# Where rows are turned in a two-layer mixture-of-experts kernel: TensorE transposes or VectorE block transposes

## The chip, the cores and the metric

One core of one Trainium2 chip runs the whole program. The metric is the device time of one execution in microseconds (us). The kernel before took 477.64 us (median of 3 runs, 476.07 to 478.81).

## The reference

```python
def reference(**kwargs):
    attn_out = _attn_ref(q, k, v, alpha)          # (2, 8, 768, 48): a gated linear recurrence
    x = attn_out.transpose(0, 2, 1, 3).reshape(B * S, H * D)        # 1536 rows of 384
    x = _moe_ref(x, w_gate, w1, w2, capacity)     # layer 1: one of 8 experts a row
    return _moe2_ref(x, w_gate, w_noise, noise, w1, w2)             # layer 2: two of 8 experts a row

def _moe_ref(...):      # per expert e, over the rows that chose it (at most 384, in order)
    out[i] = gate_w[i] * (np.maximum(x[i] @ w1[e], 0) @ w2[e])      # 384 -> 1024 -> 384

def _moe2_ref(...):     # noisy logits, the two largest, softmax of those two
    noisy_logits = logits + np.log1p(np.exp(x @ w_noise)) * noise
    out[mask] += top2_w[mask, k, None] * (np.maximum(x[mask] @ w1[e], 0) @ w2[e])
```

## The kernel before, in words

The program has three stages: the recurrence with layer 1's routing, 8 jobs of layer 1 (one per expert, numbered 0 to 7 here and `n` in the code), and 8 jobs of layer 2 (8 to 15; `E` is 8). A job is sixteen steps long. In the first eight, `hidden(n, f)` (L649) makes one block of 128 hidden units: nine products on TensorE (six in L657, three in L660: every operand is kept as a high and a low part), then ScalarE's and VectorE's high and low parts of the result (L662, L663). In the last eight, `second(n, f)` (L668, products in L686) multiplies those blocks by the second weight matrix; 72 products in all. A `hidden` result lives in one of three PSUM tiles `ph`, and is free when L662 and L663 have read it.

Beside these steps other work is issued from the same loop (L1161 on), in an order fixed by hand; there is no scheduler, so every engine runs its instructions in program order. It is:

- `raw` (L483) lets SyncE (SP) load weights two halves ahead (L492, L495), and `split` (L498) makes high and low parts of them: high on ScalarE (L510), low (L511) on VectorE or GpSimd (POOL) as `ENGS` says. `split_rest` issues the low parts one step later.
- `load_x(n)` (L572) loads the rows of job n from the store that the routing of the layer before filled by scatter (L157). `split_x(n, d)` (L597) turns a third of them, d = 0 to 2, so that features lie on partitions, and makes high and low parts. `XS` names the steps f of the second half of the job before at which this is done.
- For jobs that `turned(n)` (L559) names, which are 1 to 7 and 10 to 15, the four loads of L592 bring 32-row blocks on four groups of partitions, VectorE's 32x32 block transpose (L605) finishes the turn, and the first weight matrix is read in a copy with its rows in block order (`w1_1b`, `w1_2b`, prepared with the inputs). For the others, which are 8 and 9 (job 0 has its own way), TensorE transposes 128x128 pieces (L616) after one plain load (L569, L570). The few routing columns of a row come by a load of their own (L570, L569).
- `job_route2` and `route2` (L801, L691) route layer 2: after layer 1's job n they run in steps of the generator during job n+1, as `STEPS` says. The rank of a row among its expert's rows comes from five small products (L781 to L784, two tiles of 120 rows), then VectorE's L787 to L798, then four scatters by GpSimd.
- `finish2` (L853) ends a job of layer 2. For jobs that `turned_out(n)` (L555) names, 9 to 13, VectorE turns the result in blocks (L867), 16 loads from SBUF to SBUF by SyncE gather rows (L872), ScalarE weighs a tile of rows (L876) and GpSimd adds it to the output. For job 8 TensorE turns it back (L893).
- Rows that job 6 and 7 send late to expert 0 of layer 2 are not in job 8's block. `load_late` (L898) fetches up to 128 of them when job 7's scatters have landed, and `late_tokens` (L903) takes them through the whole expert: TensorE transposes (L908), 18 products (L920), transposes (L933), 24 products (L945). `AFTER` is the order in which the steps of `finish2(8)` (f), of `late_tokens` (l) and of `split_x(9)` (x) stand between job 8 and job 9.

```python
XS = ("135", "024", "567")     # layer 1, layer 2, job 7
AFTER = "flfflllxlxxl"
```

Of the kernel before, what the change touches and what calls it, by code (L numbers as in the profile page):

```python
# [11 lines left out]
AF = mybir.ActivationFunctionType  # L12
# [13 lines left out]
CL = 128  # L26
# [30 lines left out]
WG = 8  # L57
STEPS = ("0111122111110000", "1232210200000000", "0100000111100000", "0111000000000000")
ENGS = ("VGGGGGGGGVVVVVGV", "GGGGGGGGGGGGGGGG")
XS = ("135", "024", "567")  # L60
LATE_F = 3
AFTER = "flfflllxlxxl"
SAFE = 1e-18
LOW1, LOW2, LOW3 = C1 - 128, C2 - 128, C2 - 256

# [1 line left out]
def body(tc, ap, cap, dbg=False, stop=False):  # L67
    nc = tc.nc
    V, A, G, PE = nc.vector, nc.scalar, nc.gpsimd, nc.tensor
    with ExitStack() as ctx:  # L70
# [483 lines left out]

        def turned_out(n):  # L555

            return n > E and not by_row(n)

        def turned(n):  # L559

            return jobs[n][0] == 1 and n > 0 or place(n) is not None

        def load_rows(eng, g, rows_, c, cols):

# [7 lines left out]
        def load_x(n, eng):  # L572
            layer, e = jobs[n]
            nt_, p, c = dims(n)
            store = (xs1, xs2)[layer - 1]
            if not turned(n):
                g = sb([p, nt_, RW], "b6", 5)
                load_rows(eng, g, lambda a, b: store[e * R + a:e * R + b], c, slice(None))
            else:
                nb = -(-c // 32)  # L580
                rows_of = lambda eng, r: store[e * R:e * R + r] if layer == 1 else store[bass.ds(expert(n, eng) * R, r), :]
                w = RW if layer == 1 else RW - DM
                t6 = sb([128, nb * ND * 32 + nt_ * w], "b6", 5)
                g = t6[:p, nb * ND * 32:].rearrange("p (t d) -> p t d", t=nt_)
                if layer == 2:
                    g = few_of(g)
                load_rows(eng, g, lambda a, b: rows_of(eng.engine, nt_ * p)[a:b], c if layer == 1 else nb * 32,
                          slice(DM, None))
                x = xr_[n] = t6[:, :nb * ND * 32].rearrange("p (t d) -> p t d", t=nb)
                rows_ = rows_of(mybir.EngineType.SP, nb * 32)  # L590
                for b in range(4):
                    nc.sync.dma_start(x[b * 32:b * 32 + 32], rows_.rearrange("(t j) d -> j t d", j=32)[  # L592
                        :, :, b * ND * 32:(b + 1) * ND * 32])
            xg[n] = g
            xsp[n] = (xb([128, ND, c], F32R), xb([128, ND, c], F32R))
# [95 lines left out]
        def route2(g, yT, spare, base):  # L691
# [85 lines left out]
            V.tensor_reduce(g[:, :, NZ:NZ + E], both(wt_), axis=AX.X, op=ALU.add)  # L777
            yield
            rv = by_t(hold(nt_ * E))
            for t in range(nt_):  # L780
                PE.matmul(rv[:, t, :], tri[:p, :p], ob[:, t, :], start=True, stop=False)  # L781
                for u_ in range(t):
                    PE.matmul(rv[:, t, :], ones[:p, :p], ob[:, u_, :], start=False, stop=False)
                PE.matmul(rv[:, t, :], ones[:, :p], acc2, start=False, stop=True)  # L784
            yield
            rs = by_t(hold(nt_ * E))
            V.tensor_tensor(rs, rv, base[:p, None, :].to_broadcast(sh), op=ALU.add)  # L787
# [61 lines left out]
        def by_row(n):  # L849

            return range(3) if place(n) is not None and dims(n)[2] == 384 else None

        def finish2(n):  # L853
            nt_, p, c = dims(n)
            yp = yps.pop(n)
            if by_row(n):
                ix, ysc, group = tokens_of(xg[n], yp[0]), sb([p, nt_, DM], "b6", 5), []
                yield
                for t in range(nt_):
                    weigh(own[n], t, yp[t][:, :DM], ix, ysc, group)  # L860
                    yield
                return
            if turned_out(n):
                nb = -(-c // 32)
                z, w = sb([128, nb, ND * 32], "b6", 5), sb([128, nt_, DM], "b6", 5)
                for d in range(ND):
                    V.transpose(z[:, :, d * 32:d * 32 + 32], yp[d][:, :nb * 32].rearrange("p (t j) -> p t j", j=32))  # L867
                ix, group = tokens_of(xg[n], yp[0]), []
                yield
                for b in range(4):  # L870
                    for q in range(4):
                        nc.sync.dma_start(w[q * 32:q * 32 + 32, :len(range(q, nb, 4)), b * 96:b * 96 + 96],  # L872
                                          z[b * 32:b * 32 + 32, q::4, :])
                yield
                for t, sl, r in tiles(n):
                    A.activation(w[:r, t, :], w[:r, t, :], AF.Copy, scale=own[n][:r, t, :])  # L876
                    indirect(out, ix[:r, t:t + 1], w[:r, t, :], group, ALU.add)
                    yield
                return
            yT = sb([128, ND, c], "b6", 5)  # L880
            for d in range(ND):
                if d == 1:
                    V.tensor_copy(yT[:, d, :], yp[d][:, :c])
                else:
                    A.activation(yT[:, d, :], yp[d][:, :c], AF.Copy)
            ix = tokens_of(xg[n], yp[0])
            ysc = sb([p, nt_, DM], "b6", 5)
            yield
            group = []
            for t, sl, r in tiles(n):  # L890
                bp = ph() if n == E else pm()
                for d in range(ND):
                    PE.transpose(bp[:r, d * 128:(d + 1) * 128], yT[:, d, sl], ident)  # L893
                weigh(own[n], t, bp[:r, :DM], ix, ysc, group)
                yield


        def load_late(eng):  # L898
            g = hb([CL, 1, RW])
            eng.dma_start(g[:, 0, :], xs2[C0:C0 + CL])  # L900
            return g

        def late_tokens(n, g):  # L903

            xh, xl = xb([128, ND, CL], F32R), xb([128, ND, CL], F32R)
            xp = pm()
            for d in range(ND):
                PE.transpose(xp[:, d * CL:(d + 1) * CL], g[:, 0, d * 128:(d + 1) * 128], ident[:CL, :CL])  # L908
            m = lambda x: x.rearrange("p d c -> p (d c)")
            A.activation(m(xh), xp[:, :ND * CL], AF.Copy)  # L910
            V.tensor_tensor(m(xl), xp[:, :ND * CL], m(xh).bitcast(F32), op=ALU.subtract)
# [32 lines left out]
                for k, (l, r) in enumerate(((hh, wh), (hh, wl), (hl, wh))):  # L944
                    PE.matmul(y, l[:, sl], r, start=(f == 0 and k == 0), stop=(f == NF - 1 and k == 2))  # L945
            ysc = hb([CL, 1, DM])
            weigh(g[:, :, NZ:NZ + 1], 0, y, tokens_of(g), ysc, [])
            yield


# [214 lines left out]
        for n, (layer, e) in enumerate(jobs):  # L1165
# [3 lines left out]
            for f in range(NF):  # L1169
# [1 line left out]
                split_rest()  # L1171
                step(prev, int(steps[f]))
                if f == (3 if n == E - 1 else 0) and n not in (E, 2 * E - 1):
                    load_x(n + 1, nc.gpsimd)
                if f == 3 and turned_out(n):
                    yps[n] = {d: py() for d in range(ND)}
                    for y in yps[n].values() if dims(n)[2] % 32 else ():
# [12 lines left out]
            if n < 2 * E - 1:  # L1190
                for f in range(NF):
                    if n == E and f == LATE_F:
                        for _ in prev:
                            pass
                        g = load_late(nc.sync)
                        load_x(n + 1, nc.sync)
                        raw(n + 2, 0)
                        it = late_tokens(n, g)
                    xs_ = XS[2 if n == E - 1 else layer - 1]
                    if n != E and str(f) in xs_:  # L1200
                        split_x(n + 1, xs_.index(str(f)))
# [2 lines left out]
                        own_sums.pop()()  # L1204
                    split_rest()
                    step(prev, int(steps[8 + f]))
                    if n == E and f == 0:
                        order(2, acc2)
                    if f % 4 == 2 and (n, f) != (E, 2):
                        raw(n + 2, f // 4)  # L1210
# [15 lines left out]
                for o in AFTER if n == E else ():  # L1226
                    if o == "x":
                        split_x(n + 1, d)
                        d += 1
                    else:  # L1230
                        step(prev if o == "f" else it)
            else:
# [230 lines left out]
```

## Time and profile before

| what | value |
|---|---|
| runs | 477.64 us median, 476.07 to 478.81 |
| profiled execution | 473.87 us, its span 472.2 us |
| TensorE products (PE) | 456.6 us busy, 97% of the span, 3374 instructions |
| TensorE weight loads (PEld) | 428.6 us, 91% |
| GpSimd (POOL) | 333.0 us, 71% |
| VectorE (DVE) | 288.9 us, 61% |
| ScalarE (ACT) | 263.3 us, 56% |
| mean granted TensorE clock | 0.995 of full speed |

A busy share is an average over three stages with different limits. Times in rows are us from the start of the span. A row of a timeline gives start, duration, engine, line, operation, the tile written and the tiles read, how many instructions of that kind were merged, and in square brackets how long the engine had been idle and who released it.

### The profile page before, as it was taken

What the parts mean: (1) busy time and instruction counts of PE and PEld (TensorE: products, weight loads), DVE (VectorE), ACT (ScalarE), POOL (GpSimd) and SP (SyncE); (2) the same over time, 40 slices, a digit from 0 to 9 for tenths busy, and PEclk for the clock granted to TensorE, in tenths of its full rate; (3) what the DMA queues carried; (4) which work ended last, traced back from release to release, by engine and by line L of the source; (5) the groups of instructions that cost most, each with busy time, mean ns of one, the idle gap of its engine ahead of it and who ended that gap; (6) DMA issues with size and microseconds to landing.
All of it is one profiled execution on the core that took longest, in us unless ns stands there. A gap on an engine that the chain in (4) does not pass through costs nothing.

```text
span 472.2 us, 9805 instructions
## 1 busy us (share of the span) xinstructions
PE 456.6 (97%) x3374; PEld 428.6 (91%) x3374; DVE 288.9 (61%) x905; ACT 263.3 (56%) x683; POOL 333.0 (71%) x424
## 2 busy tenths in 40 slices
PE   8999999999999999999899999999999999999992
PEld 3688888899999999999898799999999999999992
DVE  7999988566887888888865334333442433332440
ACT  3477778377676676675553347356372555653510
POOL 3435497574777796796668219988979898696952
PEclk9999999999999999999999999999999999999997
DMA  8973863789989897786552883539377592956253
GB/s 293 408 241 143 320 235 107 254 258 307 311 307 243 264 302 219 201 290 206 175 199 59 249 210 74 122 69 336 74 254 158 142 270 55 297 104 178 37 61 48
DMA packets 73418, 95.41 MB, mean 202 GB/s; under 512 B 31261, under 2 KB 56142, under 8 KB 73358
## 3 DMA queue, kind: packets, MB, share of 16 engines
q1 hardware_dynamic: 66094, 80.54, 55.5%
q0 software_dynamic: 7264, 14.15, 12.8%
q8 instruction: 28, 0.46, 0.4%
q14 instruction: 32, 0.26, 0.2%
HBM read 70.72 MB, written 20.65 MB: 194 GB/s over the span
## 4 chain that ended last, share of the span: by engine, by line
PE 78%; DVE 11%; issue 3%; ACT 2%; DMA 2%; POOL 1%; SPq 0%; POOLq 0%; DVEq 0%
PE py L686 32%; PE ph L657 20%; PE ph L660 10%; DVE h L663 2%; PE pm L367 2%; PE ph L291 2%; DVE s L511 2%; PE py L338 2%; PE py L344 2%; PE pm L714 2%; PE py L318 1%; PE ph L920 1%; DMA s<-qs 1%; PE py L945 1%; PE py L285 1%
## 5 line engine op out<-in xcount | busy, mean ns | idle before, releaser
L511 POOL TENSOR_TENSOR s<-s,s 128x384 fp32r<-128x384 f32 x188 | 198.0, 1161 | 23.4 <-ACT s L510 19.0
L686 PE MATMUL py<-h,s 128*128 128x240 f32 (+5 forms) x1008 | 147.4, 305 | 0.0
L686 PEld LDWEIGHTS py<-h,s 128*128 128x128 f32 x1008 | 142.6, 189 | 1.3
L657 PE MATMUL ph<-x,s 128*128 128x240 f32 (+6 forms) x768 | 134.4, 310 | 0.8 <-ACT x L643 0.6
L510 ACT ACTIVATE s<-s 128x384 fp32r<-128x384 f32 x256 | 125.0, 516 | 3.9 <-DMA s<-w 2.5
L657 PEld LDWEIGHTS ph<-x,s 128*128 128x128 f32 x768 | 116.7, 189 | 2.7 <-ACT x L643 1.0
L663 DVE SCALAR_TENSOR_TENSOR h<-ph,h 128x240 fp32r<-128x240 f32 (+6 forms) x128 | 62.0, 485 | 84.8 <-ACT h L662 83.7
L662 ACT ACTIVATE h<-ph 128x240 fp32r<-128x240 f32 (+6 forms) x128 | 55.4, 433 | 79.8 <-PE ph L660 79.5
L660 PE MATMUL ph<-x,s 128*128 128x240 f32 (+6 forms) x384 | 76.8, 308 | 0.0
L157 POOL DMA_INDIRECT out<-b,m_ix x29 | 45.0, 1552 | 32.5 <-ACT b L876 7.7
L660 PEld LDWEIGHTS ph<-x,s 128*128 128x128 f32 x384 | 61.2, 189 | 0.4
L157 POOL DMA_INDIRECT xs<-b,m_si x32 | 33.8, 1057 | 21.6 <-DVE pm L797 13.7
L511 DVE TENSOR_TENSOR s<-s,s 128x384 fp32r<-128x384 f32 x68 | 48.0, 712 | 0.3 <-issue 0.2
L300 POOL TENSOR_SCALAR_AFFINE_SELECT h<-h 128x512 f32<-128x512 f32 x24 | 23.0, 980 | 27.4 <-ACT h L299 27.3
L609 DVE TENSOR_TENSOR x<-pm,x 128x240 fp32r<-128x240 f32 (+5 forms) x39 | 18.8, 482 | 26.3 <-ACT x L608 26.3
L608 ACT ACTIVATE x<-pm 128x240 fp32r<-128x240 f32 (+5 forms) x39 | 16.6, 426 | 21.0 <-DVE pm L605 17.6
L686 PE MATMUL py<-s,h 128*128 128x384 f32 x144 | 25.8, 338 | 0.0
L686 PEld LDWEIGHTS py<-s,h 128*128 128x128 f32 x144 | 25.2, 188 | 0.0
L867 DVE STREAM_TRANSPOSE b<-py 128x416 f32<-128x416 f32 (+1 forms) x15 | 8.8, 630 | 22.8 <-PE py L686 22.8
L605 DVE STREAM_TRANSPOSE pm<-b 128x256 f32<-128x256 f32 (+3 forms) x39 | 20.5, 526 | 0.0
L238 DVE TENSOR_TENSOR s<-s,s 112x256 f32<-112x256 f32 (+2 forms) x24 | 19.3, 824 | 1.4 <-DMA s<-qs 0.8
L155 POOL MEMSET spacer<- 1x1 f32 x74 | 20.1, 272 | 0.1
(253 smaller groups left out, 541.4 us busy)
## 6 DMA issues: line engine op xcount, KB each, us to landing
s<-w SPq DMA_DIRECT2D x28, 768.0 KB, 6.4
s<-w_2b SPq DMA_DIRECT2D x22, 768.0 KB, 6.6
s<-w_1b SPq DMA_DIRECT2D x14, 768.0 KB, 6.9
xs<-s SPq DMA_DIRECT2D x2, 1576.0 KB, 7.5
out<-s SPq DMA_DIRECT2D x4, 768.0 KB, 8.3
b<-xs SPq DMA_DIRECT2D x28, 96.0 KB, 6.3
b<-xs SPq DMA_DIRECT2D x12, 156.0 KB, 6.0
b<-b SPq DMA_DIRECT2D x52, 36.0 KB, 1.9
```

The source lines that it names most:

```text
L155: G.memset(spacer, 0.0)
L157: st = G.indirect_dma_start(out=dst, out_offset=bass.IndirectOffsetOnAxis(ap=ix, axis=0), in_=src, in_offset=None, **kw)
L238: eng.tensor_tensor(o, src[:, h].rearrange("r (s j) -> r s j", j=64), x[:, h].rearrange("r (s j) -> r s j", j=64), op=ALU.mult)
L300: G.affine_select(a_, a_, pattern=[[0, 4], [1, 128]], compare_op=ALU.is_ge, fill=0.0, base=0, channel_multiplier=-1)
L510: A.activation(hi[sl], t[sl], AF.Copy)
L511: rest.append(lambda: (eng or V).tensor_tensor(lo[sl], t[sl], hi[sl].bitcast(F32), op=ALU.subtract))
L605: V.transpose(y.rearrange("p (t j) -> p t j", j=32), x)
L657: PE.matmul(p, w, x[:, d, :], start=(k == 0), stop=False)
L660: PE.matmul(p, w1_of(n, f, d)[0], xl[:, d, :], start=False, stop=(d == ND - 1))
L662: A.activation(hh, p, AF.Relu)
L663: V.scalar_tensor_tensor(hl, p, 0.0, hh.bitcast(F32), op0=ALU.max, op1=ALU.subtract)
L686: PE.matmul(out_, l, r, start=(f == 0 and k == 0), stop=(f == NF - 1 and k == 2))
```

## The change

- `turned(n)` is true for every job but 0, so jobs 8 and 9 are loaded in blocks and turned by VectorE. `turned_out` takes job 8 in as well, so its result is turned by VectorE and gathered by 16 loads. Late rows are loaded by four block loads and one for their routing columns, and VectorE turns them.
- `load_x` for jobs 1 to 8 gives the load of the routing columns to SyncE (before: GpSimd).
- `split_x(8)` stands at steps 2, 4 and 6 of job 7's second half (before: 5, 6, 7).
- The five rank products of `route2` become three: one over both tiles with `tri`, one for the second tile, one over both with the running count.
- `order(2, acc2)` stands one step later in job 8, and `AFTER` is another string.

```diff
-XS = ("135", "024", "567")
+XS = ("135", "024", "246")
-AFTER = "flfflllxlxxl"
+AFTER = "llflfllxxxl"
...
-            return n > E and not by_row(n)
+            return n >= E and not by_row(n)
...
-            return jobs[n][0] == 1 and n > 0 or place(n) is not None
+            return n > 0
...
-            for t in range(nt_):
-                PE.matmul(rv[:, t, :], tri[:p, :p], ob[:, t, :], start=True, stop=False)
-                for u_ in range(t):
-                    PE.matmul(rv[:, t, :], ones[:p, :p], ob[:, u_, :], start=False, stop=False)
-                PE.matmul(rv[:, t, :], ones[:, :p], acc2, start=False, stop=True)
+            PE.matmul(rv, tri[:p, :p], ob, start=True, stop=False)
+            for t in range(nt_ - 1):
+                PE.matmul(rv[:, t + 1:, :], ones[:p, :p], ob[:, t:t + 1, :].to_broadcast([p, nt_ - 1 - t, E]),
+                          start=False, stop=False)
+            PE.matmul(rv, ones[:, :p], acc2[:, None, :].to_broadcast([128, nt_, E]), start=False, stop=True)
...
         def load_late(eng):
-            g = hb([CL, 1, RW])
-            eng.dma_start(g[:, 0, :], xs2[C0:C0 + CL])
-            return g
+            g, x, rows_ = hb([CL, 1, RW - DM]), hb([128, CL // 32, ND * 32]), xs2[C0:C0 + CL]
+            for b in range(4):
+                eng.dma_start(x[b * 32:b * 32 + 32], rows_.rearrange("(t j) d -> j t d", j=32)[
+                    :, :, b * ND * 32:(b + 1) * ND * 32])
+            eng.dma_start(g[:, 0, :], rows_[:, DM:])
+            return few_of(g), x
...
             for d in range(ND):
-                PE.transpose(xp[:, d * CL:(d + 1) * CL], g[:, 0, d * 128:(d + 1) * 128], ident[:CL, :CL])
+                V.transpose(xp[:, d * CL:(d + 1) * CL].rearrange("p (t j) -> p t j", j=32), x[:, :, d * 32:d * 32 + 32])
...
-            weigh(g[:, :, NZ:NZ + 1], 0, y, tokens_of(g), ysc, [])
+            A.activation(ysc[:, 0, :].rearrange("p (b d j) -> p d b j", b=4, d=ND),
+                         y.rearrange("p (d b j) -> p d b j", b=4, d=ND), AF.Copy, scale=g[:, 0, NZ:NZ + 1])
+            indirect(out, tokens_of(g)[:, 0:1], ysc[:, 0, :], [], ALU.add)
...
-                    load_x(n + 1, nc.gpsimd)
+                    load_x(n + 1, nc.sync if n < E else nc.gpsimd)
...
-                    if n == E and f == 0:
+                    if n == E and f == 1:
                         order(2, acc2)
...
                     if o == "x":
                         split_x(n + 1, d)
+                        split_rest()
                         d += 1
+                        while d == ND and rest:
+                            split_rest()
```

SyncE's queue around job 7, before: the second weights of job 8 (`s_687`, `s_708`), the first and then the second weights of job 9, and the late rows. The rows of job 8 were loaded from GpSimd's queue.

```order
L492 DMA s_667_3603<-w_2 128x3x512
L495 DMA s_687_3694<-w_2 128x4x384
L495 DMA s_708_3786<-w_2 128x4x384
L492 DMA s_720_3860<-w_2 128x3x512
L492 DMA s_726_3935<-w_2 128x3x512
L495 DMA s_746_4036<-w_2b 128x4x384
L495 DMA s_767_4127<-w_2b 128x4x384
L900 DMA h_4213<-xs_65 128x394
```

The same place with the change:

```order
L492 DMA s_667_3591<-w_2b 128x3x512
L495 DMA s_687_3682<-w_2b 128x4x384
L569 DMA b_691_3702<-xs_65 64x10
L570 DMA b_691_3702<-xs_65 128x2x10
L592 DMA b_691_3702<-xs_65 32x10x96 x4
L495 DMA s_708_3778<-w_2b 128x4x384
L492 DMA s_721_3853<-w_2b 128x3x512
L492 DMA s_727_3924<-w_2b 128x3x512
L495 DMA s_746_4020<-w_2b 128x4x384
L495 DMA s_770_4117<-w_2b 128x4x384
L901 DMA h_4199<-xs_65 32x4x96 x4
```

Six loads of job 8's rows, which read the store that the scatters fill, now stand on SyncE's queue between the two halves of job 8's second weights.

ScalarE's queue from the late rows' results to job 9's first blocks, before (`ysc` of job 8 is `b_787`; L844 weighs a tile out of PSUM):

```order
L936 ACTIVATE h_4338<-pm_4333 128x512
L620 ACTIVATE x_4219<-pm_4342 128x432
L936 ACTIVATE h_4354<-ph_4349 128x512
L620 ACTIVATE x_4219<-pm_4358 128x432
L620 ACTIVATE x_4219<-pm_4365 128x432
L844 ACTIVATE h_4397<-py_4372,h_4213 128x384
L844 ACTIVATE b_787_4282<-ph_4407,b_691_3714 48x384
L662 ACTIVATE h_4424<-ph_4414 128x432
```

The same place with the change (`b_793` is the tile that the 16 loads of L872 fill):

```order
L939 ACTIVATE h_4334<-pm_4329 128x512
L939 ACTIVATE h_4343<-ph_4338 128x512
L608 ACTIVATE x_4213<-pm_4347 128x432
L608 ACTIVATE x_4213<-pm_4350 128x432
L608 ACTIVATE x_4213<-pm_4354 128x432
L950 ACTIVATE h_4384<-py_4359,h_4198 128x3x4x32
L876 ACTIVATE b_793_4290<-b_793_4290,b_691_3702 128x384
L662 ACTIVATE h_4407<-ph_4397 128x432
```

In front of job 9's first L662, where ScalarE weighed a tile out of PSUM, it now weighs one that lies in SBUF and that 16 loads must have filled.

## Rows read from the trace of the kernel before

**Rows 1.** The page, its parts 1 and 2: busy time, and the granted clock.

```profile
PE 456.6 (97%) x3374; PEld 428.6 (91%) x3374; DVE 288.9 (61%) x905; ACT 263.3 (56%) x683; POOL 333.0 (71%) x424
...
PEclk9999999999999999999999999999999999999997
```

**Rows 2.** Timeline of TensorE, second half of job 7 to job 8's first block.

```profile
230.22 0.17 PE L781 MATMUL pm<-accs,tri 120*120 120x8 bf16 x1
...
230.47 2.26 PE L686 MATMUL py<-h,s 128*128 128x240 f32 x18
...
236.00 0.60 PE L616 MATMUL pm<-iw,b 128*128 128x128 f32 x3 [1.46 <-DVE accs L798]
...
239.26 1.00 PE L657 MATMUL ph<-x,s 128*128 128x304 f32 x6
...
240.52 1.64 PE L714 MATMUL pm<-iw,b 128*120 128x144 f32 x12
```

**Rows 3.** Timeline of GpSimd in the same stretch.

```profile
226.56 0.58 POOL L569 DMA_DIRECT2D b<-xs  x1 [2.15 <-issue]
...
227.93 5.88 POOL L511 TENSOR_TENSOR s<-s,s 128x384 fp32r<-128x384 f32 x6
```

**Rows 4.** Timeline of VectorE in the same stretch.

```profile
230.29 4.40 DVE L511 TENSOR_TENSOR s<-s,s 128x384 fp32r<-128x384 f32 x2
234.62 0.17 DVE L787 TENSOR_TENSOR pm<-pm,eb 120x16 f32<-120x16 f32 x1
...
235.69 0.17 DVE L798 CAST accs<-pm 120x8 bf16<-120x8 f32 x1
...
236.66 0.54 DVE L511 TENSOR_TENSOR s<-s,s 128x384 fp32r<-128x384 f32 x1
```

**Rows 5.** Groups by line and shape on VectorE: the block transposes.

```profile
L605 DVE STREAM_TRANSPOSE pm<-b 128x256 f32<-128x256 f32 x21 | 9.5, 453 | 0.0
...
L605 DVE STREAM_TRANSPOSE pm<-b 128x416 f32<-128x416 f32 x9 | 5.6, 617 | 0.0
```

**Rows 6.** Line L592, the block loads: duration of an issue on SyncE, time to landing.

```profile
L592 SPq DMA_DIRECT2D b<-xs x52: 311/450/5372, 95.2 to 408.7; - x52
...
DMA to landing us min/median/max: 2.4/7.8/13.0
```

**Rows 7.** Timeline of TensorE, from job 7's rank products to job 9's fourth block.

```profile
251.74 0.17 PE L781 MATMUL pm<-accs,tri 120*120 120x8 bf16 x1 [0.16 <-DVE m_wt L776]
...
263.19 0.52 PE L908 MATMUL pm<-iw,h 128*128 128x128 f32 x3 [0.21 <-DMA h<-xs]
...
264.29 4.58 PE L920 MATMUL ph<-s,x 128*128 128x512 f32 x18
...
270.72 1.40 PE L616 MATMUL pm<-iw,b 128*128 128x128 f32 x8 [0.31 <-DVE h L937]
272.05 4.49 PE L945 MATMUL py<-s,h 128*128 128x384 f32 x24
...
276.62 1.42 PE L657 MATMUL ph<-x,s 128*128 128x432 f32 x6
...
282.00 1.34 PE L657 MATMUL ph<-x,s 128*128 128x432 f32 x6
```

**Rows 8.** Timeline of SyncE: the load of the late rows.

```profile
260.57 0.35 SPq L900 DMA_DIRECT2D h<-xs  x1
```

**Rows 9.** Timeline of ScalarE and of VectorE: an L662, an L924 and an L663.

```profile
278.66 0.53 ACT L662 ACTIVATE h<-ph 128x432 fp32r<-128x432 f32 x1 [0.85 <-PE ph L660]
...
267.22 0.42 DVE L924 TENSOR_SCALAR h<-ph 128x256 f32<-128x256 f32 x1 [1.88 <-ACT h L926]
...
279.22 0.61 DVE L663 SCALAR_TENSOR_TENSOR h<-ph,h 128x432 fp32r<-128x432 f32 x1 [5.26 <-ACT h L662]
```

**Rows 10.** Timeline of SyncE: the sixteen loads L872 after job 9.

```profile
305.90 10.39 SPq L872 DMA_DIRECT2D b<-b  x16
```

**Rows 11.** The page, its part 6: such loads, KB each, time to landing.

```profile
b<-b SPq DMA_DIRECT2D x52, 36.0 KB, 1.9
```

More of the change, by code (lines that the diff above doesn't have):

```diff
@@ L580, in load_x @@
                 nb = -(-c // 32)
-                rows_of = lambda eng, r: store[e * R:e * R + r] if layer == 1 else store[bass.ds(expert(n, eng) * R, r), :]
+                rows_of = lambda eng, r: store[e * R:e * R + r] if layer == 1 else store[e * R:e * R + r] if place(n) is None else store[bass.ds(expert(n, eng) * R, r), :]
                 w = RW if layer == 1 else RW - DM
@@ L890, in finish2 @@
             for t, sl, r in tiles(n):
-                bp = ph() if n == E else pm()
+                bp = pm()
                 for d in range(ND):
@@ L898, in load_late, with late_tokens @@
         def load_late(eng):
-            g = hb([CL, 1, RW])
-            eng.dma_start(g[:, 0, :], xs2[C0:C0 + CL])
-            return g
-        def late_tokens(n, g):
+            g, x, rows_ = hb([CL, 1, RW - DM]), hb([128, CL // 32, ND * 32]), xs2[C0:C0 + CL]
[4 more added lines that the diff above has]
+            return few_of(g), x
+        def late_tokens(n, g, x):
             xh, xl = xb([128, ND, CL], F32R), xb([128, ND, CL], F32R)
@@ L1197, in body @@
                         raw(n + 2, 0)
-                        it = late_tokens(n, g)
+                        it = late_tokens(n, *g)
                     xs_ = XS[2 if n == E - 1 else layer - 1]
```

## The prediction
> **What bounds the kernel now.** I read the page first, for which engine is never idle; then TensorE's timeline through the two places that the change rewrites; then the timelines of the engines that feed it there. TensorE is busy for 456.6 of the 472.2 us, and its granted clock is at the upper of its two levels (2.4 GHz) in all slices but the last [rows 1]. So an instruction taken off TensorE is worth its own duration, unless something else becomes late in its place; work taken off GpSimd, VectorE or SyncE is worth nothing by itself. The places are these. At the end of job 7 TensorE turns job 8's rows in three groups of three transposes, and before the second it waits 1.46 us for VectorE; job 8's first block runs from 239.26 to 240.52 [rows 2]. VectorE was late because two of its L511 took 4.40 us beside six L511 of GpSimd [rows 3, 4] (one takes 0.54 elsewhere), and GpSimd had bunched those six because it had stood until 226.56 before it could load job 8's rows, which job 5's scatters write. Between jobs 8 and 9 TensorE first waits 0.21 us for the late rows, and then runs transposes, the late rows' products and job 9's transposes almost without a gap [rows 7].
>
> **The change, part by part.**
>
> *Rank products.* Five take 230.47 - 230.22 = 0.25 us [rows 2]; three should take 0.15. That is 0.10 us in each of 8 jobs, 0.8 in all, 0.7 of it before job 8. I expect no change of VectorE's work behind them.
>
> *Row loads of layer 1 on SyncE, seven issues off GpSimd.* Nothing waits for GpSimd there, and SyncE gets one more issue of some 0.45 us [rows 6] a job, ahead of four that wait for the same data. Cost and gain nothing; if this cover were gone, SyncE's weight loads would come 0.45 us later in a job of 18 us.
>
> *Job 8's rows.* Removed from TensorE: nine transposes (0.6 us for three at most, so 1.6) and the 1.46 us wait. With the 0.7 from above, job 8's first block could end at 240.52 - 1.46 - 1.6 - 0.7 = 236.8, a gain of 3.8; this is the upper end. Added is a chain on other engines. The loads still have to wait for job 5's scatters: 226.56 [rows 3], less 0.5 for five jobs' shorter ranks, so 226.1. SyncE issues six at 0.45, the last at 228.35. Landing took 2.4 us at least and 7.8 in the median [rows 6]. I take 2.5, since the large weight load of this moment now stands behind these loads; so the rows are there at 230.85, while the first block turn is asked for near 228.6, and VectorE's queue stands for two microseconds. From then, in the order of the program, it has: three block turns at 0.52 (between 0.453 for 256 columns and 0.617 for 416, [rows 5]), six low parts at some 0.5 [rows 4], the routing's small steps from L787 to L798, 1.24 us [rows 4], then a high part on ScalarE, a last low part and a last product, 1.1 together. The sum is 1.56 + 3.0 + 1.24 + 1.1 = 6.9 us, and job 8's first block ends at 237.75, which is 2.8 us earlier than now. With a landing of 7.8 it would end at 243.05, 2.5 us later than now; this is the lower end. The second half of job 8's second weights stands behind these loads on SyncE and lands about when its first high part is wanted; I count nothing for it. GpSimd does not bunch any more, so I expect VectorE's 4.40 us to go.
>
> By the Trainium skill, "VectorE: DVE Perf Modes", section "Rules for kernel authors", a 128x128 transpose belongs on TensorE where a PSUM destination will do, which speaks against the change. By that rule the turns would stay on TensorE and only the 0.8 us of the ranks would be gained; here TensorE is the engine without slack, so I follow the rows.
>
> *Late rows.* I count from the start of job 7's rank products (251.74 now), since the scatters and what follows them hang on those. The late load is issued 8.83 us after it (260.57, [rows 8]), and the first wide product starts 12.55 us after it (264.29, [rows 7]). With the change four loads go out, the last 1.35 us after the first, and land 2.5 after that; three turns of 128 columns take 0.32 each (the slope of [rows 5]), and the high part 0.5. The first wide product starts at 8.83 + 1.35 + 2.5 + 0.96 + 0.5 = 14.15, so 1.6 us later than now, with TensorE idle for over 3 us before it. After it the fifteen transposes of jobs 8 and 9 are gone (eight take 1.33 us, [rows 7], so 2.5), and the products wait about 0.8 us for VectorE, which turns job 8's result between the late rows' two halves. From first wide product to job 9 it is 12.33 us now, and will be 12.33 - 2.5 + 0.8 = 10.6. Job 9 starts at 24.75 after the ranks, now 24.88: about even. That `order` comes a step later, the three small memsets of job 8, and the late rows' weighing in block order lie beside TensorE's work and cost nothing.
>
> *Job 8's result.* This is what I think is late next. ScalarE weighs its first tile in front of job 9's first L662, and that tile comes by sixteen loads that go out one by one. VectorE finishes L924 3.35 us after the first wide product [rows 7, 9], then turns three times 0.52: 4.9. Sixteen issues took 10.39 us after job 9 [rows 10], 0.65 each; the last leaves at 4.9 + 15 x 0.65 = 14.65 and lands 1.9 later [rows 11], at 16.55. Then come the weighing, some 0.6, L662 0.53 and L663 0.61 [rows 9]: the first `ph` tile is free at 18.3. TensorE can run three blocks ahead and wants it for the fourth at 10.6 + 5.38 = 16.0 (5.38 is 282.00 - 276.62, [rows 7]). So it stands for 2.3 us. The fourth block starts at 14.15 + 18.3 = 32.45 after the ranks, now 30.26: 2.2 us lost, of which shorter rank products give back 0.1. The bounds are 0 (the loads are in time) and 6.3 (the late rows land in 7.8 as well).
>
> *Sum.* 2.8 - 2.2 + 0.1 = 0.7 us gained. The profiled execution took 473.87 us and would take 473.2; the median of the runs lies 3.8 us above that execution, and the forecast for the median is 477.64 - 0.7 = **476.9 us**. A measurement of this kernel can tell about 0.5% (2.4 us) from no change, so this is "no change".
>
> **The rivals.**
>
> *The sixteen loads are in time.* Everything else as above, but ScalarE does not stand. They have 14.05 - 4.9 us until they must have landed, 0.48 us an issue instead of 0.65. For it: these loads are two or three quarters of the size of those after job 9, and less else is on SyncE's queue. Against it: the 0.65 were measured on loads that differ little. Gain 2.8 + 0.1 + 0.1 = 3.0, or 4.0 with the best case for job 8's rows: 474.6, down to 473.6.
>
> *Job 8's rows come late, and the kernel gets slower.* The place is VectorE's queue at step 2 of job 7's second half: it stands until the block loads have landed, and every later low part and the routing stand behind it. The price is one microsecond for each that the landing takes over 2.5; with 3.2 the whole gain is gone, from 5.6 on the kernel is slower by over 0.5%. At 7.8, the median of L592, the time is 476.9 + 5.3 = 482.2. For it: that median. Against it: the median was taken beside weight loads in front, which are missing here.
>
> *The clock falls.* In the trace TensorE's longest wait at these places is 1.46 us, and the granted clock stayed at the upper level [rows 1, 2]; only in the last slice, after its last product, it falls. Now an idle stretch of over 3 us stands before eighteen wide products that took 4.4 us [rows 7]. At the lower level (1.2 GHz) they would take 4.4 more, and the time would be 481.3; from 1.4 us of products at that level on, the gain is gone. The Trainium skill, "TensorE: Matmul & The Clock Gate", section "Part 1: The HAM clock gate (the "warmup" mystery)", says that TensorE falls to the lower level when it has been idle and comes back after sustained work; by that rule this case would come about. No row of this trace shows a fall before the end.
>
> **How the numbers follow.** The forecast has 0.44, the sixteen loads in time 0.34, job 8's rows late 0.14, the clock 0.08. Faster by over 0.5% is the second case: 0.34. Slower by over 0.5% is the clock and most of the late rows, 0.18. Within is the rest, 0.48. The range reaches from just under the best of the second case (473.6), by the spread of a median, to the milder part of the late rows (a landing of 6): 473.0 to 480.4. The forecast alone spans 475.9 to 478.5, by landings of 2.4 to 4 and by the wait of ScalarE from 1.3 to 3 us.
>
> **What would show it.** TensorE's busy time falls by four to five microseconds, the span by less. Right: no 1.46 us wait at the end of job 7, VectorE's first turn of job 8's rows waiting for a load, job 8's first block some 2.8 us earlier; an idle stretch of about 3 us before the late products; a wait of some 2 us of TensorE at job 9's fourth block, put down to L663, with ScalarE's L876 waiting for a load just before. Wrong: no wait there (second case), L605 of job 8's rows ending after 233 (third), or a granted clock below full speed between jobs 8 and 9 (fourth).

## The result: a little slower

The changed kernel took 480.58 us (median of 9 runs, 479.78 to 482.13), the kernel before, timed beside it, 476.07 (9 runs, 475.23 to 479.54). The ratio is 1.0079, 95% interval 1.0054 to 1.0105: slower by more than 0.5%. The forecast was "no change", 476.9, with a range up to 480.4. The profiled execution took 479.78 us, its span 478.2.

The page of the changed kernel, parts 1 and 2:

```profile
PE 455.6 (95%) x3325; PEld 426.8 (89%) x3325; DVE 286.0 (60%) x918; ACT 262.0 (55%) x682; POOL 327.1 (68%) x415
...
PEclk9999999999999999999999898999999999999998
```

TensorE has 49 products fewer than in [rows 1], but only one microsecond less of busy time, where four to five were forecast. Besides the last, two slices of the clock row are below 9. The next fence says where: TensorE's timeline of the changed kernel, to be read beside [rows 2, 7].

L780 and L923 are what L781 and L920 were in the kernel before. "Job 8's ranks" are, here and below, the rank products that run during job 8 (250.72 here, 251.74 before); the prediction calls them job 7's, after the rows that they rank.

```profile
120.93 0.17 PE L780 MATMUL pm<-accs,tri 120*120 120x16 bf16 x1
...
231.92 0.17 PE L780 MATMUL pm<-accs,tri 120*120 120x16 bf16 x1
...
237.19 0.72 PE L657 MATMUL ph<-x,s 128*128 128x304 f32 x4
...
250.72 0.17 PE L780 MATMUL pm<-accs,tri 120*120 120x16 bf16 x1
...
266.42 5.73 PE L923 MATMUL ph<-s,x 128*128 128x512 f32 x18 [5.14 <-ACT x L913]
...
277.96 1.34 PE L657 MATMUL ph<-x,s 128*128 128x432 f32 x6
...
286.65 2.53 PE L657 MATMUL ph<-x,s 128*128 128x432 f32 x6 [3.23 <-DVE h L663]
```

The wait at the end of job 7 is gone; two longer ones have come, of 5.14 us before the late rows' products (L923) and of 3.23 us at job 9's fourth block. After both, TensorE works for some microseconds at the lower of its two clock levels (1.2 GHz), then at the upper one again. The windows of the changed kernel's TensorE (stretch, its length, busy time, granted clock, DMA share, GB/s):

```profile
266.40:270.00 3.60, 3.58 (x10) 0.59 1.15 199
270.00:272.20 2.20, 2.20 (x12) 1.00 1.00 313
286.60:289.20 2.60, 2.55 (x7) 0.50 1.16 240
```

Three engines' timelines show who was late: VectorE's first turn of job 8's rows (L605), by 0.19 us only; ScalarE's split of the late rows (L913) and its weighing of job 8's first tile (L876); and SyncE's loads ahead of these two.

```profile
232.27 0.53 DVE L605 STREAM_TRANSPOSE pm<-b 128x320 f32<-128x320 f32 x1 [0.19 <-DMA b<-xs]
...
265.88 0.49 ACT L913 ACTIVATE x<-pm 128x384 fp32r<-128x384 f32 x1 [14.32 <-DVE pm L911]
...
284.93 0.61 ACT L876 ACTIVATE b<-b,b 128x384 f32<-128x384 f32 x1 [6.18 <-DMA b<-b]
285.45 0.51 ACT L662 ACTIVATE h<-ph 128x432 fp32r<-128x432 f32 x1
...
261.22 1.75 SPq L901 DMA_DIRECT2D h<-xs  x4
263.08 0.37 SPq L903 DMA_DIRECT2D h<-xs  x1
...
272.31 10.41 SPq L872 DMA_DIRECT2D b<-b  x16
```

The distances between starts of TensorE's rows, in us, with a second profile of each kernel (from the experiments below); a wide product is one of the late rows' eighteen of 512 columns:

| from, to | before, first | before, second | after | after, second | forecast |
|---|---|---|---|---|---|
| job 1's ranks, job 7's | 108.88 | 111.19 | 110.99 | 110.91 | 108.3 |
| job 7's ranks, job 8's | 21.52 | 23.16 | 18.80 | 18.78 | 19.3 |
| job 8's ranks, first wide product | 12.55 | 12.56 | 15.70 | 15.53 | 14.15 |
| first wide product, job 9 | 12.33 | 12.31 | 11.54 | 12.04 | 10.6 |
| job 9's first block, fourth | 5.38 | 5.38 | 8.69 | 8.85 | 7.7 |
| fourth block, eighth | 7.09 | 7.09 | 8.60 | 8.73 | 7.1 |

From job 10's first block to the end it is 167.0 to 167.2 us in all four. (The forecast's first two entries are the first column less 0.1 for each job's ranks, and the second less the 2.1 of job 8's rows too.) The table leaves three questions: is layer 1's loss of two microseconds the change's, why do the late rows come at 15.7, and what are the two waits worth in time.

### The profile page after: what moved, and what is told of

The parts are those of the page before. It is cut to its first block, busy times and chain, and to the rows that moved or that the text cites. A ratio compares the mean times of both kernels' runs of the same rounds, so it can differ in the third digit from the quotient of the medians.

```text
span 478.2 us, 9737 instructions
## 1 busy us (share of the span) xinstructions
PE 455.6 (95%) x3325; PEld 426.8 (89%) x3325; DVE 286.0 (60%) x918; ACT 262.0 (55%) x682; POOL 327.1 (68%) x415
## 5 line engine op out<-in xcount | busy, mean ns | idle before, releaser
L511 POOL TENSOR_TENSOR s<-s,s 128x384 fp32r<-128x384 f32 x188 | 199.9, 1227 | 31.8 <-ACT s L510 31.5
L657 PE MATMUL ph<-x,s 128*128 128x240 f32 (+6 forms) x768 | 136.6, 313 | 4.5 <-DVE h L663 3.4
L663 DVE SCALAR_TENSOR_TENSOR h<-ph,h 128x240 fp32r<-128x240 f32 (+6 forms) x128 | 62.0, 485 | 91.3 <-ACT h L662 79.0
L662 ACT ACTIVATE h<-ph 128x240 fp32r<-128x240 f32 (+6 forms) x128 | 55.4, 433 | 81.9 <-PE ph L660 74.2
L660 PE MATMUL ph<-x,s 128*128 128x240 f32 (+6 forms) x384 | 77.1, 309 | 0.0
L157 POOL DMA_INDIRECT out<-b,m_ix x29 | 45.1, 1554 | 27.2 <-ACT b L876 10.7
L511 DVE TENSOR_TENSOR s<-s,s 128x384 fp32r<-128x384 f32 x68 | 42.1, 624 | 0.4 <-ACT s L510 0.3
L609 DVE TENSOR_TENSOR x<-pm,x 128x240 fp32r<-128x240 f32 (+6 forms) x45 | 22.0, 489 | 27.1 <-ACT x L608 24.2
L608 ACT ACTIVATE x<-pm 128x240 fp32r<-128x240 f32 (+6 forms) x45 | 19.5, 433 | 27.0 <-DVE pm L605 22.4
L605 DVE STREAM_TRANSPOSE pm<-b 128x256 f32<-128x256 f32 (+4 forms) x45 | 23.9, 533 | 0.2 <-DMA b<-xs 0.2
L867 DVE STREAM_TRANSPOSE b<-py 128x416 f32<-128x416 f32 (+2 forms) x18 | 10.1, 606 | 22.5 <-PE py L686 22.5
```

The source lines that it names most:

```text
L157: st = G.indirect_dma_start(out=dst, out_offset=bass.IndirectOffsetOnAxis(ap=ix, axis=0), in_=src, in_offset=None, **kw)
L511: rest.append(lambda: (eng or V).tensor_tensor(lo[sl], t[sl], hi[sl].bitcast(F32), op=ALU.subtract))
L605: V.transpose(y.rearrange("p (t j) -> p t j", j=32), x)
L609: rest.append(lambda: V.tensor_tensor(xl[:, d, :], y[:, :c], xh[:, d, :].bitcast(F32), op=ALU.subtract))
L657: PE.matmul(p, w, x[:, d, :], start=(k == 0), stop=False)
L660: PE.matmul(p, w1_of(n, f, d)[0], xl[:, d, :], start=False, stop=(d == ND - 1))
```

## Experiment 1: layer 1

Four kernels. Ranks alone: the kernel before with the new rank products. Loads alone:

```diff
-                    load_x(n + 1, nc.gpsimd)
+                    load_x(n + 1, nc.sync if n < E - 1 else nc.gpsimd)
```

Loads put back: the kernel after with `load_x(n + 1, nc.gpsimd)` at that place. And the kernel after itself once more.

> The kernel before with the three rank products alone. Measure in the profile: from job 1's rank products to job 7's, 108.88 us before (121.34 to 230.22) and 110.99 after (120.93 to 231.92). Theory A (the row loads on SyncE cost layer 1 its time): 108.88 - 6 x 0.10 = 108.3 us here, time 0.7 us under before. Theory B (the shorter rank products themselves shift VectorE and GpSimd against each other): 110 to 111 us here, time over 1 us above before. Theory C (the loss in layer 1 belongs to the execution, not to the program: ScalarE sees TensorE's products late): 108.3 us, unless its first L662 of a job waits around 1 us after its product, and the time 0.7 us under before.

> The kernel before with L570 of layer 1's jobs issued by SyncE, nothing else (job 8's loads stay with GpSimd). Same measure, 108.88 us before. Theory A: 110.5 to 111.5 us and a time 2 us above before, with GpSimd's L511 beside VectorE's at the second step of a job. Theory B: 108.9 us, time as before. Theory C: 108.9 us and time as before, unless ScalarE's first L662 of a job waits long.

> The kernel after with all of the row loads L569 and L570 back on GpSimd. Theory A: 108.3 us from job 1's ranks to job 7's, time about 2 us under the kernel after (478.5 where that is 480.6). Theory B and theory C: about 111 us and the time of the kernel after; under C the number goes with how late ScalarE's L662 starts, not with where the loads are issued. Job 8's rows may land up to 1 us later, since GpSimd's L511 stand in front of the loads again.

> The kernel after, unchanged, for a second profile. Theories A and B: 110.99 us from job 1's ranks to job 7's again, within 0.3. Theory C: the late starts of ScalarE's L662 (0.9 to 1.6 us after the product, in the profile of the kernel after) are there or not by the execution, so this distance may come out at 108.3. The scatters of job 7 should show whether their 4.6 us to landing (2.9 before) is the program's: if so L901 leaves 10.5 us after job 8's ranks again, if not 8.8.

Measured: ranks alone 476.79 us, ratio to before 1.0011 (0.9983 to 1.0040); loads alone 476.85, 1.0016 (0.9992 to 1.0039); the kernel after 480.37. From job 1's ranks to job 7's it is 110.9 to 111.1 us in all four. So neither part costs the two microseconds in time (0.42%; both intervals end at 1.0040 or below), and A and B, which would have one of these two kernels without the loss, fall: every profile but the first of before has it. The kernel after's late rows' loads left 10.57 us after job 8's ranks again, so that delay is the program's. Ranks alone show no gain of 0.7 us in the profile either (the interval of the time is too wide to tell). Loads put back took 483.1 us, 1.0126 (1.0099 to 1.0152), 2.7 above the kernel after, which none of the theories had: job 8's ranks come 0.5 us later there (19.28 after job 7's), job 9's fourth block comes 9.30 us after the first, and the low clock there lasts past the fifth (9.91 us from fourth to eighth). Job 8's loads, then, are half a microsecond better on SyncE; why the rest is lost at job 9's fourth block was not followed up.

One run was left that could tell whether the first profile of before was the odd one: the kernel before, unchanged, profiled again.

> The kernel before, unchanged, for a second profile. If its first profile was an execution unlike the others: from job 1's rank products to job 7's about 111 us as in the ten other profiles (108.88 in the first), ScalarE's first L662 of a job late, a span of 474 to 477 us. If the change and each of its parts cost layer 1 two microseconds: 108.9 again and a span of 472.

Its span is 476.0 us (477.70 for the execution), and layer 1 takes 111.19 us. Rows of it: TensorE's timeline, a window as above (here with all engines: PE, PEld, DVE, ACT, POOL, clock, DMA share, GB/s) and, of ScalarE's waits between 120 and 232 us, one (us in total, times, longest).

```profile
121.32 0.17 PE L781 MATMUL pm<-accs,tri 120*120 120x8 bf16 x1
...
232.51 0.17 PE L781 MATMUL pm<-accs,tri 120*120 120x8 bf16 x1
...
235.44 0.60 PE L616 MATMUL pm<-iw,b 128*128 128x128 f32 x3 [0.42 <-DMA b<-xs]
...
238.40 0.60 PE L616 MATMUL pm<-iw,b 128*128 128x128 f32 x3 [1.17 <-DVE accs L798]
238.93 2.19 PE L686 MATMUL py<-h,s 128*128 128x240 f32 x9
...
255.67 0.17 PE L781 MATMUL pm<-accs,tri 120*120 120x8 bf16 x1
...
240.00:243.00 3.00, 3.00 (x17) 2.58 (x16) 0.93 (x2) 1.12 (x3) 2.57 (x5) 0.59 0.89 290
...
ACT h L662 <- PE pm L714: 7.5, 6, 1.7
```

So the profile that the prediction was built on was an unusual execution of the kernel before: 473.87 us, where no timed run of that kernel, in any of these sets, came under 474.9. In it ScalarE took up TensorE's first block of a layer 1 job at most half a microsecond late. In the fourteen other profiles, of either kernel, it waits six times, up to 1.7 us, and is released only while L714 runs, behind the next block, as in the last row; the first profile has no such row. And the wait at the end of job 7 cost more than its length: after 1.17 us of it nine products of job 7 took 2.19 us, where eighteen take 2.26 in [rows 2], and the granted clock was 0.59 over the next three microseconds. With that wait and the nine transposes gone, the stretch from job 7's ranks to job 8's is 4.4 us shorter than in the second profile, 2.7 than in the first. Both kinds of profile are single executions; which of them the timed runs are nearer to, the runs do not tell.

## Experiment 2: job 9's fourth block

Weighing later leaves everything of the change and moves only ScalarE's L876, with GpSimd's addition to the output that follows each, behind the fifth, sixth and seventh L662 of job 9:

```diff
-            steps = STEPS[n // E if n <= E else 2 if turned_out(n - 1) else 3]
+            steps = "0000111000000000" if n == E + 1 else STEPS[...]
-            step(prev)
+            step(prev, n != E + 1)
```

> The kernel after, with ScalarE weighing job 8's three tiles (L876) behind its fifth, sixth and seventh L662 of job 9 instead of ahead of the first, ahead of the second and behind the last. Measure: from job 9's first block to its fourth, 8.69 and 8.85 us in the two profiles of the kernel after, 5.38 in before's; from the fourth to the eighth 8.60 and 8.73, before 7.09. If the sixteen loads L872 that stand in ScalarE's way make the wait: 5.4 and 7.1 here, no low clock at job 9's fourth block, 4.8 us under the kernel after, so about 475.6 (slightly under the kernel before). Rival (the wait is GpSimd's or SyncE's, for a buffer of the next job's rows that the result still holds): the wait moves to job 10's first blocks, and at most 1.5 us (the clock) is won.

Measured: 475.86 us (12 runs), ratio to before 0.9985 (0.9955 to 1.0015): 4.5 us under the kernel after, of 4.8 expected. TensorE, then ScalarE, of this kernel:

```profile
278.47 1.34 PE L657 MATMUL ph<-x,s 128*128 128x432 f32 x6
...
283.78 1.34 PE L657 MATMUL ph<-x,s 128*128 128x432 f32 x6
284.96 0.75 PE L660 MATMUL ph<-x,s 128*128 128x432 f32 x3
285.55 1.34 PE L657 MATMUL ph<-x,s 128*128 128x432 f32 x6
...
287.58 0.53 ACT L662 ACTIVATE h<-ph 128x432 fp32r<-128x432 f32 x1 [0.83 <-PE ph L660]
288.18 0.62 ACT L876 ACTIVATE b<-b,b 128x384 f32<-128x384 f32 x1
```

No wait before the fourth block (283.78, 5.30 after the first), full clock after it, and L876 finds its loads landed. The wait did not move on: job 10 starts 28.3 us after job 9, 28.4 before. Turning job 8's result on TensorE instead takes the sixteen loads away altogether:

```diff
-            return n >= E and not by_row(n)
+            return n > E and not by_row(n)
-                bp = pm()
+                bp = ph() if n == E else pm()
-AFTER = "llflfllxxxl"
+AFTER = "flfflllxlxxl"
```

(with the late rows' weighing in plain order again).

> The kernel after, with job 8's result turned back by TensorE as in the kernel before (nine transposes of L893, plain second weights for job 8, no L872 loads for it), its weighing split between ScalarE and VectorE. If the sixteen loads make the wait at job 9's fourth block: 5.4 us from job 9's first block to its fourth and 7.1 from the fourth to the eighth, 4.8 us won there; TensorE gets nine transposes back, some 1.3 us, partly inside its 5 us wait for the late rows. About 476.5. Rival (the late rows' own delay carries over, ScalarE is late anyway): the wait shrinks by half at most, 478.5.

> The kernel after, with job 8's result turned back by TensorE as in the kernel before, all of the late rows' steps kept (the run with this edit that came first left out their second product). If the sixteen loads L872 make the wait: 5.4 us from job 9's first block to its fourth and 7.1 from the fourth to the eighth, as in the run that weighs later; of the nine transposes that come back on TensorE six lie in its wait for the late rows, three cost about 0.5. About 476.4, half a microsecond above the run that weighs later. Rival (VectorE's turning was hiding another delay): over 477.5.

The first of the two leaves out the late rows' second product and weighing, so its 476.47 us says little. The second took 477.05 us, ratio 0.9993 (0.9957 to 1.0030); fourth block 5.38 us after the first, fourth to eighth 7.09:

```profile
280.84 1.42 PE L657 MATMUL ph<-x,s 128*128 128x432 f32 x6
...
286.23 1.34 PE L657 MATMUL ph<-x,s 128*128 128x432 f32 x6
```

The sixteen loads in ScalarE's way made the wait, shown in two ways. (Job 9 as a whole takes 29.2 us here, 28.3 with the later weighing; part of that is a wait of 0.49 us for GpSimd's L511 behind the eighth block.) By the Trainium skill, "VectorE: DVE Perf Modes", section "Rules for kernel authors", this result would stay on TensorE, which has a PSUM destination for it; VectorE's way with a later weighing is the quicker by the ratios, but by 0.0008, less than their intervals can tell apart, so no run here decides that.

## Experiment 3: why the late rows come late

In the kernel after, the late rows' loads leave 10.50 us after job 8's ranks, not 8.83, though the last scatter is issued 5.86 us after them, as before. DMA traffic of the kernel after in the stretch 258 to 260.2, by queue (packets, MB, share), shows beside the scatters' packets one that no line of the kernel issues:

```profile
q0 software_dynamic: 61, 0.18, 31.8%
q8 instruction: 1, 0.02, 4.4%
```

It carries 16 KB of instructions. The span has 28 such packets, one for some 120 of TensorE's 3325 products, so I took them for TensorE's program. Measured from job 8's ranks it starts after 7.5 us here and after 4.6 in both profiles of before; with the ranks alone changed, sixteen products fewer, after 7.0, and the late rows' load left after 9.47 there. The change, by taking products away, seemed to have put the fetch in front of the last scatter. Thirty narrow products at the very start should move it without touching anything else:

```diff
         warm(WARM0)
+        fp = ph()
+        for _ in range(30):
+            PE.matmul(fp[:, :64], wt[:, :128], wt[:, :64], start=True, stop=True)
```

> The kernel after, with thirty narrow products (128x64, results unused) behind the warming products at the start, which move the places in time at which TensorE's instructions are fetched and nothing else. In both profiles of the kernel after, a 16 KB instruction packet starts 7.5 us after job 8's rank products and takes 1.6 to 1.7 us, the last scatter's packets end 9.95 to 10.0 after them (8.4 where that packet came at 4.6 or 5.5), and the late rows' loads leave at 10.5 (8.8 to 9.0). If the fetch holds the last scatter up: loads leave at 8.8 to 9.0, first wide product at 14.1 instead of 15.6, time 1.5 us under the kernel after (less up to 0.5 for the thirty products). Rival (another cause of the scatter's landing, from the changed program): loads leave at 10.5 again, time as the kernel after plus up to 0.5.

Of this kernel (its lines stand 3 lower than the kernel after's): DMA traffic in 254 to 256, where the packet now is; SyncE; TensorE; a window of TensorE.

```profile
q8 instruction: 1, 0.02, 3.3%
...
259.98 1.75 SPq L904 DMA_DIRECT2D h<-xs  x4
...
264.88 7.09 PE L926 MATMUL ph<-s,x 128*128 128x512 f32 x18 [3.22 <-ACT x L916]
...
267.00:270.00 3.00, 3.00 (x8) 0.50 1.16 207
```

The ranks of job 8 start at 251.11 here, so the loads leave after 8.87 us and the first wide product starts after 13.77. The packet starts 3.1 us after the ranks, 4.4 earlier than before the edit, and the loads leave 1.6 us sooner. All fifteen profiles agree: where the packet starts 3.1 to 5.5 us after the ranks, the loads leave after 8.8 to 9.0; where it starts 7.4 to 8.1 after them, after 10.4 to 10.7; with the ranks alone changed both lie between. So the fetch had held the last scatter up; that it is TensorE's fits the edit, which added nothing but products, and how it holds a scatter up is not shown. The time was 479.57 us, ratio 1.0044 (1.0019 to 1.0069), 0.8 to 1.0 under the kernel after, though the intervals overlap; 1.5 were expected, but the low clock now lasted for more of the eighteen wide products (7.09 us). What the moved fetch is worth when the clock holds is in experiment 4. The clock alone: nineteen products whose result nobody uses, in that wait.

```diff
+            wp = ph()
+            for _ in range(19):
+                PE.matmul(wp, parts[n, 0][0][:, 0, :128], parts[n, 0][0][:, 0, :], start=True, stop=True)
             xp = pm()
```

> The kernel after, with nineteen products of 512 columns (results unused, about 4.7 us) on TensorE between job 8's second half and the late rows' products, where it stands 5 us. Clock theory: no fall there, the eighteen wide products take 4.2 us from the first to the last one's start instead of 5.3 to 5.8, job 9 starts 1.2 to 1.5 us sooner after job 8's ranks (26.0 instead of 27.2 to 27.6); the wait at job 9's fourth block grows by as much, since the sixteen loads go out by VectorE's L927 as before, or a little less. So the time is 0 to 1.3 us under the kernel after. Rival (the wide products wait for data, the clock matters little): no change of the 5.3, time as the kernel after.

```profile
260.75 4.50 PE L911 MATMUL ph<-s 128*128 128x512 f32 x19
265.61 4.54 PE L926 MATMUL ph<-s,x 128*128 128x512 f32 x18 [0.36 <-ACT x L916]
...
275.98 1.34 PE L657 MATMUL ph<-x,s 128*128 128x432 f32 x6
...
285.17 2.53 PE L657 MATMUL ph<-x,s 128*128 128x432 f32 x6 [3.74 <-DVE h L663]
```

The wide products take 4.54 us again, and from the first of them to job 9 it is 10.37 us, not 11.54 to 12.04. The wait at the fourth block grew by half a microsecond. 479.38 us, ratio 1.0061 (1.0039 to 1.0083): 1.0 to 1.2 under the kernel after, which the intervals alone do not tell apart. As the Trainium skill has it ("TensorE: Matmul & The Clock Gate", section "Part 1: The HAM clock gate (the "warmup" mystery)"), idling lowers the clock and work keeps it; the trace agrees (4.54 against 5.73 us for the same products).

## Experiment 4: together

> The later weighing and the nineteen filling products in the late rows' wait together. If both work on different places: no low clock between jobs 8 and 9 at all, from job 8's ranks to job 9 25.6 us (27.2 without the filling), from job 9's first block to the fourth 5.3; 475.9 - 1.5 = 474.4. Rival (a later weighing is only in time because the clock was low before it): the wait at a block of job 9 comes back, 475.5 to 476.

> The later weighing, the thirty narrow products at the start that move TensorE's instruction fetch, and twelve filling products (the wait is then 3.2 us). Loads leave 8.9 us after job 8's ranks, first wide product at 13.8, the clock holds, job 9 starts 23.9 after the ranks (27.2 in the kernel after): 475.9 - 3.3 = 472.6, plus up to 0.5 for the thirty products, so about 473, 0.7% under the kernel before. Rival (what is won in the late rows' wait is given back because ScalarE's weighing now meets its loads): 474.5 to 476.

> As the run of the three edits together, with two of the late rows' four block loads issued by ScalarE, which is idle there, so that SyncE's last issue comes 0.8 us sooner. If issuing is on the path: first wide product 0.6 to 0.8 us sooner (13.0 to 13.2 after job 8's ranks), time 0.7 us less. Rival (the landing is set by the last, small load or by the packets, not by when the loads are issued): no change.

| kernel | us | ratio to before |
|---|---|---|
| later weighing, filling | 474.32 | 0.9936 (0.9908 to 0.9964) |
| later weighing, moved fetch, filling (12 products) | 472.85 | 0.9909 (0.9880 to 0.9939) |
| the same, two late loads issued by ScalarE | 472.13 | 0.9896 (0.9843 to 0.9950) |

TensorE of the second kernel (whose ranks start at 250.97; the window ends in the third row) and, last, of the third (ranks at 251.27):

```profile
261.36 2.91 PE L914 MATMUL ph<-s 128*128 128x512 f32 x12
265.02 4.54 PE L929 MATMUL ph<-s,x 128*128 128x512 f32 x18 [0.75 <-ACT x L919]
...
275.38 0.94 PE L660 MATMUL ph<-x,s 128*128 128x432 f32 x4
...
264.90 4.58 PE L929 MATMUL ph<-s,x 128*128 128x512 f32 x18 [0.33 <-ACT x L919]
```

Each sum came out as the parts added up (474.4, 473 and 0.7 less were expected), the second with some luck: its first wide product came at 14.05 us after the ranks, not 13.8, and job 9 at 24.4, not 23.9. All three lie under the kernel before by more than their intervals, the last by 4.8 us of before's median (476.96 beside it) and by over 8 of the kernel after's. The difference between the last two lies inside their intervals; the first wide product came 0.4 us sooner (13.63 us after the ranks, not 14.05), of 0.6 to 0.8 expected. The moved fetch holds for this instruction count alone.

## Why the prediction was wrong

- **Rank products: 0.7 us before job 8. Wrong, nothing gained that the profiles can tell.** From job 1's ranks to job 7's it is 111.07 us with the new products alone, 111.19 and 111.05 in two profiles with the old ones. In the kernel after, the first product waits 0.2 to 0.3 us for VectorE (L776) in five of the eight jobs, but so it does in the second profile of before; where the tenth of a microsecond goes stays open.
- **Row loads on SyncE cost and gain nothing. Right** (loads alone 1.0016).
- **Job 8's rows. Right in kind.** The wait went, VectorE's first turn waited for its load, and from there to the end of job 8's first block it took 7.0 us, 6.9 forecast. The term, 2.1 us without the ranks, measured 2.7 against the profile that it was made from, and 4.4 against the second one, in which the clock fell too. No run has this part alone.
- **Late rows: "the late load is issued 8.83 us after it". This step failed first.** It was 10.50, and the rest of the sum held: 1.35 and 2.5 for issue and landing, 1.46 for turns and split make 5.3, measured 5.20. With the fetch moved, the loads left at 8.87 and the first wide product came at 13.77, 14.15 forecast; that is still 1.2 us later than before (12.55), which is what the block loads and the turns cost. What failed was to take the scatter's landing over as if it hung on the scatters alone.
- **From there to job 9, 10.6 us.** 10.37 with the clock held, 11.5 to 12.0 as it was. The rival "the clock falls", at 0.08, was no rival but part of the forecast's own course: it named an idle stretch of over 3 us and then priced what followed at full clock. Even with the fetch moved, and the wait 3.22 us as forecast, the clock fell. That rival's time, 481.3, lies near the measured one by luck: of its 4.4 us the wide products lost 1.2 to 1.7.
- **Job 8's result: a wait of 2.3 us. Right in mechanism, too small.** Measured 3.23. The sixteen issues took the 10.4 us forecast, but the first left 5.9 us after the first wide product instead of 4.9, and the tile had landed at 284.85, 18.4 after it instead of 16.55: the last took 2.7 us to land, not the 1.9 taken from [rows 11]. The late start was the clock's: with the clock held by the filling products alone, the first left after 4.7 us.
- **Nothing was set down for what this wait does to the clock.** The fourth block's six products took 2.53 us instead of 1.34, and 1.5 us were lost by the eighth.
- **The base.** The forecast for the median used the difference between one profile and the median and took it for constant. The profile had been an odd execution, so gains were measured from a kernel two microseconds faster in layer 1 than any other profile shows. The median itself, 477.64 of three runs, was 476.07 with nine.
- **Small slips in the working.** The eighteen wide products took 4.58 us [rows 7], not 4.4. In the rival of the sixteen loads in time, 16.0 less 1.74 for weighing, L662 and L663 is 14.2, not 14.05. The bound of 6.3 on the loss at job 9 does not follow from its terms: with a landing of 7.8 for 2.5 the same sum loses 2.2 + 5.3 = 7.5. None of them changes the forecast.

The table's differences against the second profile are +0.2, +4.4, -3.1, +0.8, -3.3 and -1.5, 2.6 us lost (unrounded); against the first they make 6.6; the medians say 4.5. Between these two lies the part of the timed runs that the profiles leave open. The chance for "slower", 0.18, was too low because the clock was kept apart as a rival, though the forecast's own idle stretch brought it about: the low clock put off the sixteen loads, and the wait that they made took the clock down again.

## What to carry to other kernels

Here a transfer chain that ended ahead of an activation in the program's order stopped everything behind it on ScalarE: before anything is turned elsewhere, move the consumer behind the next work it doesn't feed (this alone gave 4.5 us). If a forecast contains an idle stretch of TensorE like those here (3.2 to 5.1 us), price the products after it at the lower clock, and fill the stretch if it can't be closed. And profile the kernel before twice: the first profile was 2.3 us shorter in layer 1 and 1.6 us shorter at the end of job 7 than the second.

## What the hardware showed that was not expected

- Fetching instructions can hold up the kernel's own DMAs: with one 16 KB packet ahead of the last scatter's, the loads that wait for the scatter left 1.6 us later, and thirty products more at the start of the program moved the packet out of the way.
- ScalarE took up a block up to 1.7 us late in layer 1's jobs in fourteen profiles of fifteen. What decides this was not found.
- A wait of 1.46 us left the clock up in one profile of before [rows 1, 2]; in the other the clock fell after waits of 0.42 and 1.17 us.
